# Linear attention and a gated feed-forward on one core: scores and tiled outputs of two batches in one stretch, halves in steps 1 and 2, later planned landings, last rows in two parts

## The chip, the core and the metric

The kernel runs on one core of a Trainium2 chip. Its engines have instruction streams of their own: PE (matrix products, TensorE), ACT (ScalarE), DVE (VectorE), POOL (GpSimd) and SP (SyncE, which here only starts transfers). PEld in the profile is PE's loading of weights. The metric is device time in microseconds (us); lower is better. Eight runs of the kernel before lie between 198.23 and 200.33 us, with a median of 199.31.

## What is computed

```python
B, H, S, D = 4, 8, 768, 48          # q, k, v, f_logit: [B, H, S, D]
f = sigmoid(f_logit)
for t in range(S):
    state = f[:, :, t, :, None] * state + einsum('bhd,bhe->bhde', k[:, :, t], v[:, :, t])
    y[:, :, t] = einsum('bhd,bhde->bhe', q[:, :, t], state)
x = y.transpose(0, 2, 1, 3).reshape(B * S, H * D)            # 3072 x 384
out = (maximum(x @ w_gate, 0) * (x @ w_val)) @ w_out         # hidden width 1536
```

## The kernel before

**Tiling.** The sequence is cut into six steps of 128 tokens (`c`, 0 to 5). In a step each of the four batches is a unit of attention, and two batches form a pair (`pr`, 0 or 1). The recurrence is computed by blocks: sums of log f over the tokens of a step (`cum`, L659 and L662; L573 and L593 in step 0), exponentials of them on ACT (L669, L671), scaled k and q ("hats", L696 and L699 on POOL), their transposes `qkT` (on PE, L710, with a DVE copy L715 in steps 1 and 2; by a transposing DMA, L718, from step 3 on), scores k·q (L739), the causal mask (`ptm`, L744 on DVE), the output rows (L766 or L772/L776) and the new state (L800, then L548 on DVE and L550 on POOL).

**Two kinds of small-tile stretches on PE.** Scores contract over 48 rows, and heads are stored at row 0 and row 64, so a batch's eight score matmuls alternate between the two halves of PE's rows and fill two banks of PSUM. The "tiled" outputs of steps 0 to 2 (`intra`, L766) write 32 partitions at a time: 16 matmuls per batch, plus 12 with the old state from step 1 on. They give the outputs already transposed, as the feed-forward wants them. From step 3 on (`natural`) the outputs are 128 rows wide and a transposing DMA (L791) turns them.

**Feed-forward.** For each of twelve blocks of hidden units (`j`) `ffn_hidden` computes gate and value, three matmuls each (L829); ACT takes relu of the gate (L835), DVE multiplies (`gT`, L839). A triple of three matmuls is 512 columns wide, or 256 where `halves` splits the four batches: for the first six `j` of step 0 each half of the batches has triples of its own. `ffn_out` multiplies twelve blocks of `gT` by w_out (L852, 384 columns), ACT evicts (L862), SP stores 128 rows (L866).

**What sets the order.** Nothing is placed by hand. Every operation is put into a plan with the tiles that it reads and writes, an assumed cost (`occ`, `lat`) and a priority. `schedule` takes, again and again, the operation that can start first (priority breaks ties) and so makes a fixed order for each engine; it also deals out the eight PSUM banks, at most so many of a kind (four of "f" for the feed-forward, four of "s" for scores, two of "y"). `settle` repeats this eight times, and between the rounds `transfers` plays the two DMA queues (SP's and POOL's) packet by packet to get a planned landing for each load. On the chip each engine works its list in order and waits on semaphores. Planned times thus decide only who stands behind whom. `dma` (L446) holds what `transfers` needs: packets and ns per packet, alone and beside the other queue. Attention comes before feed-forward by priority, and chains (`chain`, L513) keep scores, outputs, transposes and feed-forward matmuls each in their own order.

**Transfers.** SP loads f, k, q, v, one pair at a time (384 KB each); POOL starts the loads of w_gate, w_val and w_out in three parts each (L494), which also convert to bf16. The list `first` (L318) fixes the first of them: `wo0@q1.0` lets part 0 of w_out start only when q of step 1, pair 0 has landed; `f1.0@wv1` holds that f until part 1 of w_val has landed. Part s of w_out is read by the s-th four of the twelve L852 matmuls of a row block.

**Filling.** In the first 15 us PE gets idle matmuls (L912) on planned gaps.

Of the kernel before, what the change touches and what calls it, by code (L numbers as in the profile page):

```python
# [42 lines left out]
class Plan:  # L43
# [140 lines left out]
    def transfers(self):  # L184
# [9 lines left out]
        for op in rings["POOL"]:  # L194
            queue["POOL"].append([op, op.parts[0], op.start + 3.0])
# [24 lines left out]
        while True:  # L220
            feed()
            heads = {e: queue[e][0] for e in queue if queue[e]}
            if not heads:
                break
            can = {e: h for e, h in heads.items() if h[2] <= t}
            if not can:
                times = [h[2] for h in heads.values()]
                if nxt < len(sp) and pending is None:
                    times.append(max(sp[nxt].ready, issue["SP"]))
                t = max(t + 0.01, min(times))  # L230
                continue
            e = next(iter(can)) if len(can) == 1 else ("POOL" if last == "SP" else "SP")
            h = can[e]
            t += h[0].parts[1 if len(can) == 1 else 2] / 1000.0
            last = e
            h[1] -= 1
            if e == "SP":
                sent += 1
            if h[1] == 0:
                h[0].land = t + (0.6 if e == "SP" else 1.6)  # L240
                queue[e].pop(0)
# [58 lines left out]
def bass_hgrn2_outer__then__ffn_reglu_kernel(  # L300
# [12 lines left out]
    halves = {0: 6}  # L313
    dec_dma = set()
    x_way = {0: "tiled", 1: "tiled", 2: "tiled", 3: "xbar", 4: "xbar", 5: "xbar"}
# [5 lines left out]
    C = 128  # L321
# [30 lines left out]
    dec = [sb(f"dec{i}", [128, B // 2, 2, 2, NP], F32) for i in range(NA)]  # L352
    NW = 2
    drow = sb("drow", [128, NW, D, 2, 2, NP], F32)
# [31 lines left out]
    def pe_t(*cols):  # L386
        return sum({256: 0.124}.get(n, n / 2400.0 + 0.0045) for n in cols)
# [58 lines left out]
    def dma(op, slot, flow, parts, n=1):  # L446
# [5 lines left out]
        op.flow, op.parts = flow, (n * parts[0], parts[1], parts[2])  # L452
# [31 lines left out]
    def load_w(nm, s, after):  # L484
# [12 lines left out]
        dma(op, f"{nm}{s}", 2.45, (32, 62, 62) if nm == "wo" else (24, 80, 80))  # L497
# [40 lines left out]
    def new_state(kv, c, b, w, P):  # L538
        ai = c % NA
        s_old, s_new = st[b][(c + 1) % 2], st[b][c % 2]  # L540
        rate = dec[ai][:, b // 2, :, b % 2, :].rearrange("q j p -> q p j").unsqueeze(3).to_broadcast([128, NP, 2, D])
# [11 lines left out]
    def attention_pair(c, b0):  # L553
# [43 lines left out]
        for j in range(2):  # L597
            lo = 64 * j
            add("ACT", lambda lo=lo, j=j: sc.activation(
                dec[ai][lo:lo + 64, b0 // 2, j, :, :].rearrange("p b n -> p n b"),  # L600
# [39 lines left out]
    def attention_front(c, b):  # L640
# [17 lines left out]
        def cum():  # L658
            mm = te.matmul(bc.ap[:, 0:HD], tri[:, :], bn[:, :, 0:D])  # L659
            if c < NC - 1 and c not in dec_dma:  # L660
# [4 lines left out]
        chain("cum", "PE", cum, ["tri", "ones", f"bneg{bi}", f"bn{bi}_{bj}"], [bc], occ=0.28 if c < NC - 1 and c not in dec_dma else 0.17,  # L665
# [7 lines left out]
        if c in dec_dma:  # L673
            wi = w // 2 % NW
            add("ACT", lambda: sc.activation(drow[96:128, wi, :, :, bj, :].rearrange("q d j p -> q p j d"),
                                             bc.ap[96:128, 0:HD].rearrange("q (p j d) -> q p j d", p=NP, j=2), AF.Exp, scale=-1.0),
                [bc], [f"drow{wi}_{bj}"], prio=P + 2, **act_t(HD))
            if bj:
                def copies():
                    row, cell = NW * 2 * HD, 2 * B * NP  # L680
                    return [sy.dma_start(
                        bass.AP(tensor=dec[ai], offset=64 * j * cell + (b // 2) * 4 * NP + j * 2 * NP, ap=[[cell, D], [1, 2 * NP]]),
                        bass.AP(tensor=drow, offset=127 * row + wi * 2 * HD + j * 2 * NP, ap=[[row, 1], [4 * NP, D], [1, 2 * NP]]))
                        for j in range(2)]
                op = add("SP", copies, [f"drow{wi}_{i}" for i in range(2)] + [f"dec{ai}"],
                         [f"dec{ai}_{b_}{j}{hh}" for b_ in (b - 1, b) for j in range(2) for hh in range(2)], occ=0.9, lat=1.2, prio=P + 5)
                dma(op, f"dec{ai}_{b // 2}", 0.2, (3, 16, 24), 2)
        elif c < NC - 1:
            for j in range(2):
                lo = 64 * j  # L690
                add("ACT", lambda lo=lo, j=j: sc.activation(dec[ai][lo:lo + 64, b // 2, j, bj, :], bc.ap[lo:lo + 64, HD:HD + NP], AF.Exp,
# [31 lines left out]
    def attention(c, b):  # L723
        w = c * B + b
        P = w * 10
        hi, qi, mi, vi = w % NH, w % NQ, w % NM, w % NV
        xi = c % NX
        vp = vpad[vi]
        vin = ld["v"][:, slot_of("v", c, b // 2), b % 2, :, :]
        vout = bass.AP(tensor=vp, offset=0, ap=[[VW, 128], [VSTEP, NP], [64, 2], [1, D]])  # L730
        add("POOL", lambda: gp.tensor_copy(vout, vin.rearrange("p (n j) d -> p n j d", j=2)),  # L731
            in_keys("v", c, b, b + 1) + [f"vpad{vi}"], [f"v_{vi}"], prio=P + (55 if c in twos else 3), **pool_c(HD))
        sA, sB = Bank("s"), Bank("s")

        def scores():
            for p in range(NP):
                for j, s in ((0, sA), (1, sB)):
                    lo = 64 * j
                    mm = te.matmul(s.ap[:, p * C:(p + 1) * C], tokens(c, b, 1, p, lo, lo + D), tokens(c, b, 0, p, lo, lo + D))  # L739
            return mm  # L740
        chain("scores", "PE", scores, qk_(qi), [sA, sB], occ=0.34, lat=PE_L, prio=P + 5, opens=[sA, sB])
        mask = tri[:].unsqueeze(1).to_broadcast([128, NP, C])
        for j, s in ((0, sA), (1, sB)):
            add("DVE", lambda j=j, s=s: ve.tensor_tensor(  # L744
                ptm[mi][:, j, :, :], s.ap[:, :].rearrange("p (n t) -> p n t", n=NP), mask, ALU.mult),
                [s, "tri"], [f"ptm{mi}_{j}{hh}" for hh in range(2)], prio=P + 6, **dve_t(512))

        y = Bank("y")
        s_old = st[b][(c + 1) % 2]
        s_key = [f"S{b}_{(c + 1) % 2}"] if c else []  # L750

        def intra():
# [6 lines left out]
            for r in range(NK):  # L759
                rounds.append([(n, vp[:, p * VSTEP + 32 * i + 16 * (i == 2):p * VSTEP + 32 * i + 16 * (i == 2) + 32],  # L760
                                ptm[mi][:, i // 2, p, :]) for n, (p, i) in list(enumerate(blocks))[4 * r:4 * r + 4]])
            rounds.append([(3 * p + 1, vp[:, p * VSTEP + 48:p * VSTEP + 80], ptm[mi][:, 1, p, :]) for p in range(NP)])
# [7 lines left out]
        def natural():  # L770
# [3 lines left out]
            for h in range(H):  # L774
                at = h // 2 * VSTEP + h % 2 * 64
                mm = te.matmul(y.ap[:, h * D:(h + 1) * D], ptm[mi][:, h % 2, h // 2, :], vp[:, at:at + D],  # L776
                               start=False, stop=True, skip_group_check=True)
            return mm
        x_key = [f"xT{xi}_{b}"]
        need = qk_(qi) + [f"v_{vi}", *(f"ptm{mi}_{j}{hh}" for j in range(2) for hh in range(2))] + s_key  # L780
        if x_way[c] == "tiled":
            yop = chain("intra", "PE", intra, need + [f"vpad{vi}"], [y], occ=0.52 if c else 0.38, lat=PE_L, prio=P + 7, opens=[y])
            add("ACT", lambda: sc.activation(xT[xi][:, :, b * C:(b + 1) * C],  # L783
                                             y.ap[:, 0:HD].rearrange("p (n t) -> p n t", n=NK), AF.Copy),
                [y], x_key, prio=P + 8, **act_t(HD))
        else:
            chain("intra", "PE", natural, need, [y], occ=0.38, lat=PE_L, prio=P + 7, opens=[y])
            ni = w % NN
            add("ACT", lambda: sc.activation(xn[ni][:, :], y.ap[:, 0:HD], AF.Copy), [y], [f"xn{ni}"], prio=P + 8,
                **act_t(HD))  # L790
            op = add("SP", lambda: sy.dma_start(xT[xi][:, :, b * C:(b + 1) * C], xn[ni][:, :], transpose=True),  # L791
                     [f"xn{ni}"], x_key, prio=P + 8, occ=1.3, lat=1.2)
            dma(op, f"xT{xi}_{b}", 0.6, (24, 20, 28))

        def rest():
            kv = Bank("kv")

            def state():
                for p in range(NP):
                    mm = te.matmul(kv.ap[:, p * 96:(p + 1) * 96],  # L800
                                   hats[:, hi, 1, 2 * p:2 * p + 2, :].rearrange("p h d -> p (h d)"),
                                   bass.AP(tensor=vp, offset=p * VSTEP, ap=[[VW, 128], [64, 2], [1, D]]))
                return mm
            if c in twos:
                attention_back(c, b, behind[-1])
            chain("state", "PE", state, hk_(hi) + [f"hats{hi}", f"v_{vi}"], [kv],
                  occ=0.18, lat=PE_L, prio=P + (32 if c in twos else 6), opens=[kv])
            new_state(kv, c, b, w, P + (25 if c in twos else 0))
        if c in twos:
            behind.append(yop)  # L810
            later.append(rest)
        elif c < NC - 1:
            rest()
# [28 lines left out]
    OJ = 4  # L842

# [28 lines left out]
    for c in range(NC):  # L872
# [5 lines left out]
        for b in range(B):  # L878
            if c not in twos and b % 2 == 0:
                attention_front(c, b)  # L880
                attention_front(c, b + 1)
            elif b % 2 == 0:
                attention_pair(c, b)
            attention(c, b)
# [13 lines left out]
    for item in pend:  # L898
        ffn_out(*item)

# [102 lines left out]
```

## Time and profile before

| | us |
|---|---|
| median of 8 runs | 199.31 |
| lowest, highest | 198.23, 200.33 |
| the profiled execution | 199.21 |
| its span, first to last instruction | 197.5 |
| busy in it: PE, PEld | 186.2, 102.4 |
| busy in it: ACT, DVE, POOL | 111.1, 105.4, 76.2 |
| eight score matmuls, mean duration of one | 0.218 |
| four maskings in a row on DVE, at 20.92 us | 2.48 |

The span is what the trace shows; the rest of an execution lies around it. Matmuls overlap: the duration of one is longer than its share of PE's time, so the share is read from start to next start. The DMA engines are busy through most of the first 134 us:

```profile
0.00:5.00 5.00, 3.45 (x9) 1.05 (x10) 3.71 (x13) 1.50 (x2) 3.96 (x17) 1.00 0.51 138
30.00:36.20 6.20, 3.97 (x29) 2.10 (x30) 2.75 (x6) 4.62 (x15) 2.84 (x4) 1.00 1.04 199
36.20:62.00 25.80, 25.80 (x333) 15.18 (x334) 15.85 (x27) 17.02 (x38) 17.95 (x23) 1.00 1.11 213
91.00:134.00 43.00, 43.00 (x349) 23.01 (x349) 21.91 (x34) 26.29 (x56) 17.82 (x22) 1.00 0.94 187
134.00:186.60 52.60, 52.60 (x334) 26.93 (x333) 22.11 (x33) 23.19 (x43) 4.83 (x6) 1.00 0.28 72
```

Each row is a stretch of the span: its length, the busy time (and number of instructions) of PE, PEld, DVE, ACT and POOL, the granted TensorE clock, the busy share of the DMA engines and GB/s.

### The profile page before, as it was taken

The numbers are of one execution on the slowest core, as the hardware profiler recorded it, in microseconds if no ns is written. First come the engines' busy times: TensorE is split into PE (matmuls) and PEld (weight loads), VectorE is DVE, ScalarE is ACT, GpSimd is POOL, SyncE is SP. The second block draws the span as 40 slices with busy tenths as digits, with TensorE's granted clock in tenths as the row PEclk, the third lists the DMA queues.
The fourth block names the chain that finished last, engine by engine and source line by source line (L and its number), as shares of the span: only waits on it lengthen the run. The fifth ranks groups of instructions, "written<-read, shape, count | busy, mean of one in ns | idle before, by whom it ended". The sixth has DMA issues, their size and how long they took to land.

```text
span 197.5 us, 4253 instructions
## 1 busy us (share of the span) xinstructions
PE 186.2 (94%) x1705; PEld 102.4 (52%) x1705; DVE 105.4 (53%) x183; ACT 111.1 (56%) x237; POOL 76.2 (39%) x108
## 2 busy tenths in 40 slices
PE   6874997799999999999999999999999999999994
PEld 2443784356655554556455555544545555544562
DVE  7755874574819786576566455446247232443300
ACT  2776439671587768856646876377434434344311
POOL 8276002976286829594640652904500000000000
PEclk9999999999999999999999999999999999999999
DMA  4999999999999989997899979999562210111112
GB/s 136 272 271 205 206 194 204 182 206 216 221 208 242 204 174 219 193 230 150 191 174 186 236 169 181 210 194 228 106 132 62 61 40 0 43 40 40 40 75 84
DMA packets 118051, 31.73 MB, mean 161 GB/s; under 512 B 111120, under 2 KB 118032, under 8 KB 118032
## 3 DMA queue, kind: packets, MB, share of 16 engines
q1 hardware_dynamic: 114048, 27.93, 66.3%
q0 software_dynamic: 3984, 3.54, 11.1%
q8 instruction: 13, 0.21, 0.4%
q14 instruction: 6, 0.05, 0.1%
HBM read 25.95 MB, written 4.72 MB: 155 GB/s over the span
## 4 chain that ended last, share of the span: by engine, by line
PE 80%; issue 8%; POOL 5%; DMA 3%; SPq 2%; ACT 0%; POOLq 0%
PE ps L829 43%; PE ps L852 24%; PE ps L739 3%; DMA f_in<-in_f_logit_dram 3%; PE ps L766 2%; PE ps L710 2%; SPq L474 2%; PE ps L659 2%; PE ps L800 2%; POOL wg L494 1%; PE ps L776 1%; POOL wv L494 1%; PE ps L772 1%; POOL vpad L731 1%; PE ps L662 1%
## 5 line engine op out<-in xcount | busy, mean ns | idle before, releaser
L839 DVE TENSOR_TENSOR gT<-relu,ps 128x512 bf16<-128x512 bf16 (+1 forms) x78 | 49.8, 644 | 58.3 <-PE ps L829 47.8
L835 ACT ACTIVATE relu<-ps 128x512 bf16<-128x512 f32 (+1 forms) x78 | 43.7, 563 | 30.2 <-PE ps L829 29.9
L829 PE MATMUL ps<-xT,wv 128*128 128x512 bf16 (+1 forms) x234 | 59.5, 363 | 1.1 <-DMA wv<-in_moe_w_val_dram 1.1
L829 PE MATMUL ps<-xT,wg 128*128 128x512 bf16 (+1 forms) x234 | 59.4, 363 | 0.6 <-DMA wg<-in_moe_w_gate_dram 0.6
L852 PE MATMUL ps<-wo,gT 128*128 128x384 bf16 x288 | 51.4, 326 | 0.0
L744 DVE TENSOR_TENSOR ptm<-ps,tri 128x512 bf16<-128x512 f32 x48 | 30.9, 683 | 11.7 <-PE ps L739 11.7
L852 PEld LDWEIGHTS ps<-wo,gT 128*128 128x128 bf16 x288 | 27.0, 98 | 18.7
L829 PEld LDWEIGHTS ps<-xT,wg 128*128 128x128 bf16 x234 | 21.7, 98 | 20.3 <-issue 0.7
L829 PEld LDWEIGHTS ps<-xT,wv 128*128 128x128 bf16 x234 | 21.1, 98 | 20.8 <-DMA wv<-in_moe_w_val_dram 1.4
L696 POOL TENSOR_TENSOR hats<-k_in,expo 128x384 bf16<-128x384 f32 x20 | 19.9, 1002 | 27.4 <-ACT expo L669 15.4
L862 ACT ACTIVATE osb<-ps 128x384 f32<-128x384 f32 x24 | 11.8, 491 | 31.3 <-PE ps L852 31.3
L699 POOL TENSOR_TENSOR hats<-q_in,expo 128x384 bf16<-128x384 f32 x20 | 19.9, 1000 | 1.9 <-DMA q_in<-in_q_dram 1.9
L550 POOL TENSOR_TENSOR st<-ssum,dec 128x384 bf16<-128x384 f32 x16 | 13.6, 847 | 10.7 <-DVE ssum L548 10.7
L731 POOL CAST vpad<-v_in 128x384 bf16<-128x384 f32 x24 | 11.9, 507 | 4.5 <-DMA v_in<-in_v_dram 4.5
L669 ACT ACTIVATE expo<-ps 128x384 f32<-128x384 f32 x20 | 9.8, 490 | 3.8 <-PE ps L662 3.0
L650 ACT ACTIVATE f_in<-f_in 128x768 f32<-128x768 f32 x10 | 8.4, 840 | 4.0 <-DMA f_in<-in_f_logit_dram 4.0
L548 DVE TENSOR_TENSOR ssum<-ps,st 128x384 f32<-128x384 f32 x16 | 8.8, 552 | 3.3 <-PE ps L800 2.9
L739 PE MATMUL ps<-qkT 48*128 48x128 bf16 x192 | 9.2, 218 | 0.9 <-ACT qkT L617 0.9
L671 ACT ACTIVATE expo<-ps 128x384 f32<-128x384 f32 x20 | 9.8, 488 | 0.0
L739 PEld LDWEIGHTS ps<-qkT 48*128 48x128 bf16 x192 | 5.4, 94 | 7.9 <-issue 5.0
L783 ACT ACTIVATE xT<-ps 128x384 bf16<-128x384 f32 x12 | 5.9, 490 | 5.0 <-PE ps L766 4.9
L715 DVE COPY qkT<-ps 128x1024 bf16<-128x1024 bf16 x8 | 5.5, 690 | 5.7 <-PE ps L710 5.7
(73 smaller groups left out, 143.2 us busy)
## 6 DMA issues: line engine op xcount, KB each, us to landing
f_in<-in_f_logit_dram SPq DMA_DIRECT2D x12, 384.0 KB, 5.1
k_in<-in_k_dram SPq DMA_DIRECT2D x12, 384.0 KB, 5.3
q_in<-in_q_dram SPq DMA_DIRECT2D x12, 384.0 KB, 6.0
v_in<-in_v_dram SPq DMA_DIRECT2D x12, 384.0 KB, 5.4
out_dram<-osb SPq DMA_DIRECT2D x24, 192.0 KB, 2.4
wg<-in_moe_w_gate_dram POOLq DMA_DIRECT2D x3, 384.0 KB, 8.0
wv<-in_moe_w_val_dram POOLq DMA_DIRECT2D x3, 384.0 KB, 9.2
wo<-in_moe_w_out_dram POOLq DMA_DIRECT2D x3, 384.0 KB, 7.9
```

Of the source, the lines that this page charges most:

```text
L550: add("POOL", lambda: gp.tensor_tensor(t4(s_new), t4(tmp), rate, ALU.mult), [key] + dk, [f"S{b}_{c % 2}"], prio=P + 8, **pool_t(HD))
L669: add("ACT", lambda: sc.activation(ex[:, 1, :], bc.ap[:, 0:HD], AF.Exp, scale=1.0), [bc], [f"expk{ei}"], prio=P + 1, **act_t(HD))
L696: add("POOL", lambda: gp.tensor_tensor(hk, kin[:, b % 2, :, :], ex[:, 1, :].rearrange("p (h d) -> p h d", h=H), ALU.mult), in_keys("k", c, ...
L699: add("POOL", lambda: gp.tensor_tensor(hq, qin[:, b % 2, :, :], ex[:, 0, :].rearrange("p (h d) -> p h d", h=H), ALU.mult), in_keys("q", c, ...
L731: add("POOL", lambda: gp.tensor_copy(vout, vin.rearrange("p (n j) d -> p n j d", j=2)), in_keys("v", c, b, b + 1) + [f"vpad{vi}"], [f"v_{v ...
L739: mm = te.matmul(s.ap[:, p * C:(p + 1) * C], tokens(c, b, 1, p, lo, lo + D), tokens(c, b, 0, p, lo, lo + D))
L744: add("DVE", lambda j=j, s=s: ve.tensor_tensor(ptm[mi][:, j, :, :], s.ap[:, :].rearrange("p (n t) -> p n t", n=NP), mask, ALU.mult), [s, " ...
L829: mm = te.matmul(bank.ap[:, 0:n], wt[:, kt, j * 128:(j + 1) * 128], xT[xi][:, kt, n0:n1], start=(kt == 0), stop=(kt == NK - 1))
L835: add("ACT", lambda: sc.activation(relu[ri][:, 0:n], gate.ap[:, 0:n], AF.Relu), [gate], [f"relu{ri}"], prio=P, **act_t(n))
L839: add("DVE", lambda: ve.tensor_tensor(gT[gi][:, j, n0:n1], relu[ri][:, 0:n], val.ap[:, 0:n], ALU.mult), [val, f"relu{ri}"], [f"gT{gi}_{j}_ ...
L852: mm = te.matmul(o[b].ap[:, 0:DM], gT[gi][:, j, b * C:(b + 1) * C], wo[:, j, :], start=(j == 0), stop=(j == NJ - 1))
L862: add("ACT", lambda b=b, oi=oi: sc.activation(osb[oi][:, :], o[b].ap[:, 0:DM], AF.Copy), [o[b]], [f"osb{oi}"], prio=P, **act_t(DM))
```

## The change

`attention` takes both batches of a pair. For the pairs in `s_twin` (all but the first pairs of steps 0 and 1) their sixteen score matmuls are one operation that opens four banks; for those in `y_twin` ((1,1), (2,0), (2,1)) the tiled outputs of both batches are one operation with two banks. Which pairs have tiled outputs stays the same. `halves` now covers steps 1 and 2 too. In the plan, landings on SP's queue are put 1.0 or 1.9 us after the last packet (before 0.6), POOL's transfers begin 2.2 or 2.9 us after their start (before 3.0), wo's packets take 80 ns beside the other queue (before 62), and PE's assumed costs are a table. The rows of the last batch of the last step go through `ffn_end`: columns 0 to 255, then 256 to 383, each with its own bank, eviction and store. A path for decays by DMA, used in no step, is removed, and `dec` is laid out so that the decays of one batch lie together.

```diff
-            queue["POOL"].append([op, op.parts[0], op.start + 3.0])
+            queue["POOL"].append([op, op.parts[0], op.start + op.parts[3]])
...
-                h[0].land = t + (0.6 if e == "SP" else 1.6)
+                h[0].land = t + (1.6 if e == "POOL" else 1.0 if h[0].ready < 1.0 else 1.9)
...
-    halves = {0: 6}
-    dec_dma = set()
-    x_way = {0: "tiled", 1: "tiled", 2: "tiled", 3: "xbar", 4: "xbar", 5: "xbar"}
+    halves = {0: 6, 1: 6, 2: 6}
+    x_way = {(c, pr): "tiled" if c < 3 else "xbar" for c in range(6) for pr in range(2)}
+    s_twin = {(c, pr) for c in range(6) for pr in range(2)} - {(0, 0), (1, 0)}
+    y_twin = {(1, 1), (2, 0), (2, 1)}
...
-        return sum({256: 0.124}.get(n, n / 2400.0 + 0.0045) for n in cols)
+        return sum({128: 0.0566, 256: 0.109, 384: 0.1627, 512: 0.2162}[n] for n in cols)
...
-        dma(op, f"{nm}{s}", 2.45, (32, 62, 62) if nm == "wo" else (24, 80, 80))
+        dma(op, f"{nm}{s}", 2.45, (32, 62, 80, 2.2) if nm == "wo" else (24, 80, 80, 2.9))
...
-    def attention(c, b):
...
-        chain("scores", "PE", scores, qk_(qi), [sA, sB], occ=0.34, lat=PE_L, prio=P + 5, opens=[sA, sB])
+    def attention(c, bs):
+        units = []
...
+        for part in ([units] if (c, bs[0] // 2) in s_twin else [[u] for u in units]):
+
+            def scores(part=part):
+                for b, w, s in part:
+                    for p in range(NP):
+                        for j in range(2):
+                            lo = 64 * j
+                            mm = te.matmul(s[j].ap[:, p * C:(p + 1) * C], tokens(c, b, 1, p, lo, lo + D),
+                                           tokens(c, b, 0, p, lo, lo + D))
+                return mm
+            at = [s for _, _, ss in part for s in ss]
+            chain("scores", "PE", scores, [t for _, w, _ in part for t in qk_(w % NQ)], at, occ=0.21 * len(part) + 0.22, lat=PE_L,
+                  prio=part[0][1] * 10 + 5, opens=at)
...
+        for part in ([units] if tiled and (c, bs[0] // 2) in y_twin else [[u] for u in units]):
+            ys = [Bank("y") for _ in part]
+
+            def rows(part=part, ys=ys):
+                return [(intra if tiled else natural)(u, y) for u, y in zip(part, ys)][-1]
+            op = chain("intra", "PE", rows, [t for u in part for t in need(u) + ([f"vpad{u[1] % NV}"] if tiled else [])], ys,
+                       occ=(0.34 if c else 0.19) * len(part) + 0.235 if tiled else 0.38, lat=PE_L, prio=part[0][1] * 10 + 7, opens=ys)
...
+    def ffn_end(g, b, cols):
+        gi, oi = g % NG, (g * B + b) % NO
+        P = (g + 1) * B * 10 + 5 + NJ * 3 + b * 3
+        for i, (n0, n1) in enumerate(cols):
+            o = Bank("f")
+
+            def part(o=o, n0=n0, n1=n1):
+                for j in range(NJ):
+                    mm = te.matmul(o.ap[:, 0:n1 - n0], gT[gi][:, j, b * C:(b + 1) * C], wo[:, j, n0:n1], start=(j == 0),
+                                   stop=(j == NJ - 1))
+                return mm
...
-        for b in range(B):
-            if c not in twos and b % 2 == 0:
+        for b in range(0, B, 2):
+            if c in twos:
+                attention_pair(c, b)
+            else:
                 attention_front(c, b)
                 attention_front(c, b + 1)
-            elif b % 2 == 0:
-                attention_pair(c, b)
-            attention(c, b)
+            attention(c, (b, b + 1))
...
-    for item in pend:
+    for item in pend[:-1]:
         ffn_out(*item)
+    ffn_end(NC - 1, B - 1, [(0, 256), (256, DM)])
```

## The prediction

> **What bounds the kernel now.** First the page: does one engine fill the span, and where not?
>
> ```profile
> span 197.5 us, 4253 instructions
> PE 186.2 (94%) x1705; PEld 102.4 (52%) x1705; DVE 105.4 (53%) x183; ACT 111.1 (56%) x237; POOL 76.2 (39%) x108
> PE   6874997799999999999999999999999999999994
> PEclk9999999999999999999999999999999999999999
> ```
>
> PE is full from about the eighth slice (8 x 4.94 = 39 us) to the end, at full clock; the others are about half busy. Holes are only in the head. Second, the chain that ended last, in order of time (start, length, what):
>
> ```profile
> 18.29 15.04 issue
> ...
> 33.34 0.81 POOL wo L494
> 34.16 1.01 POOL hats L696
> 35.17 0.95 POOL hats L699
> 36.17 0.62 PE ps L710 x8
> ...
> 186.80 7.81 PE ps L852 x48
> 194.64 0.49 ACT osb L862
> ```
>
> Until 36.17 POOL decides: it stands still until q of step 1, pair 0 has landed (the waits give 15.05 us to that DMA), issues wo part 0 and makes two hats, and PE starts step 1's transposes. From there the chain is PE alone to 194.64, and the PE waits after 36.2 us list no other wait at all. So the time is: head (36.17), plus every PE slot after it (158.5), plus a tail of 2.85 (eviction 0.49, store issue 0.33, landing 1.8, the end). The profiled execution took 199.21, 1.72 more than its span; the median of eight is 199.31, so the sum needs no shift.
>
> Third, the PE timeline, for what a slot costs. I read start to next start, not the durations, since matmuls overlap:
>
> ```profile
> 20.39 0.63 PE L739 MATMUL ps<-qkT 48*128 48x128 bf16 x16
> 20.95 0.50 PE L829 MATMUL ps<-xT,wg 128*128 128x256 bf16 x3
> ...
> 38.09 0.81 PE L829 MATMUL ps<-xT,wg 128*128 128x512 bf16 x3
> 38.84 0.40 PE L739 MATMUL ps<-qkT 48*128 48x128 bf16 x8
> 39.17 0.34 PE L659 MATMUL ps<-bneg,tri 128*128 128x384 bf16 x1
> ```
>
> Three 512-wide matmuls take 0.648 in a row, but 0.75 before scores: 0.10 is lost on entering. Eight scores take 0.33, sixteen 0.56: eight more cost 0.23, so 0.10 of the 0.33 is lost on leaving. Tiled outputs (L766) show the same: 12 in 0.175, so 16 should take 0.233, yet they take 0.33; entering costs 0.09. I call this a switch, 0.097 mean.
>
> **Part 1: scores of two batches together, tiled outputs of two together.** In the instruction order of the two kernels I count entries and exits of the two kinds of small-tile stretches: 65 before, 42 after. Scores go from 20 stretches of 8 and two of 16 to two of 8 and eleven of 16; outputs of (1, pair 1) and both pairs of step 2 merge. The matmuls are the same. 23 fewer switches x 0.097 = **2.23 us** off PE, all behind 47 us, where PE is full. The Trainium skill has a rule for this (TensorEngine Tiling (Array Packing), Key Properties): changing the tiling mode drains TensorE. It gives no price; as an estimate, TensorE: Matmul & The Clock Gate, Single matmul latency, puts an isolated 128-wide warm matmul at (398+128)/2.4 = 219 ns, 163 more than the 56 of a streamed one (eight transposes take 0.45), so 23 switches would bring 3.7 us. The trace has its own row for a switch, so I take 2.23.
>
> The cost side is DVE. Both batches' scores fill four banks, and their four maskings (L744) are placed in one run nearly everywhere: four took 2.48 us at 20.92, two took 1.29. Behind them on DVE queue the products into gT (L839), which free PE's banks. A rule speaks against the change here: the tiling page, PSUM Bottleneck, warns that faster tiles leave evacuation as the limit. By the rule each twin is worth DVE's 2.48, not PE's 0.56 + 0.10. By the trace, DVE is idle 47% of the time, and what counts is the PE work placed behind the scores. Worst place: step 1, pair 1. The first gT can start 0.53 (scores to masking) + 2.4 + 0.5 (a state sum) = 3.4 us after the scores start; PE has 0.56 + 0.17 (state) + 0.54 (sums) + 7 x 0.327 = 3.56 us of work to the point at which four products are open. So it just fits. Elsewhere 1.95 us blocks of w_out follow, needing no DVE. Bounds for all twins: 0 to 9 x 0.3 = 2.7; below nothing is excluded, since no row lets a longer burst free a bank earlier. I take **+0.5**, near the place worked out.
>
> **Part 2: halves for steps 1 and 2.** 72 matmuls of 512 columns become 144 of 256: 48 x 0.327 - 24 x 0.648 = **+0.15** on PE. ACT and DVE each get 12 more instructions: 12 x (2 x 0.382 - 0.596) = 2.0 and 12 x (2 x 0.415 - 0.686) = 1.7 us, beside PE; their cover is the idle half, and what it costs when gone is in the burst bounds above. It also lets step 1's hidden layer start with two batches instead of four (before: last xT at 56.2, first use at 56.86).
>
> **Part 3: later planned landings, new PE costs.** These only reorder. In the head, PE gets two more half triples and a full one ahead of step 1's sums, and in all three more full triples ahead of its transposes (3 x 0.648 = 1.95 us net), where before it stood 1.36 (29.22 to 30.91, less 0.33) and 1.47 us (34.05 to 36.17, less 0.65). ACT lets one more relu pass before the exponential that waits for f (landing at 29.0). POOL's gate is the same transfer: SP's first 17 issues are unchanged, wv part 1 (landing 14.06 + 9.2 = 23.2) still releases them, so the transposes still start at about 36.17. POOL puts a vpad before wg part 0 (into its 1.35 us of waiting) and a hats before wv part 2, whose use is far off: nothing.
>
> So 1.95 would be gained, but what is late next? The w_out matmuls now come earlier. The landings of wo parts 0, 1, 2 are 33.3+6.3, 36.5+7.9, 37.3+9.7 = 39.6, 44.4, 47.0. Adding slots from 36.17 in the new order, PE reaches part 1 at 43.94 (waits 0.46) and part 2 at 46.3 (waits 0.7): it goes on at 47.0, where before it was at the same point at 47.80. Of 1.95 only **0.80** stays. This also swallows any small stall in the head up to 1.15.
>
> SP: the first two stores of step 0 move ahead of k and q of step 2, and SP waits for their eviction (48.3, 48.9). k then goes out at about 49.7 (before 46.81), q at 51.2 (48.30), v at 52.8 (53.40), f of pair 1 at 56.4 (53.91). With landings of 6.4 and 6.1 (the k and q rows at 46.8 and 48.3) q is there at 57.3, its hats done by 59; PE wants them at 59.6. Covered by 0.6 us. Later loads fall within 2 us of the old ones while PE's score stretches come 1 to 4 us later than before.
>
> **Part 4: last rows in two parts.** 12 x 384 columns (1.95) become 12 x 256 and 12 x 128: 1.31 + 0.68 = 1.99, +0.03. The last eviction shrinks from 0.49 to about 0.27 (256 columns take 0.38, so 0.11 less per 128); the first store's issue (0.33) is over before the second is ready. The smaller transfer may land 0.1 sooner than 1.8. **-0.28** in all.
>
> **Sum.** 199.21 - 2.23 + 0.5 + 0.15 - 0.80 - 0.25 (tail with its PE cost) = **196.6**.
>
> **Rivals.** *B, wo does not bind* (0.12): its parts land 1.2 us earlier, since the queues run differently. Then all of the 1.95 stays: 195.4. Against it: POOL issues them at the same gate and the same loads compete. *C, the DVE burst decides* (0.15): each twin costs PE 0.3: 196.6 - 0.5 + 2.7 = 198.8, no measurable change. For it: 2.48 us against banks for about 2.6 us of hidden layer. Against: in the old kernel DVE waits 47.8 us for L829's matmuls, PE none for DVE. *D, stores ahead of loads* (0.13), the slower one: q of step 2 behind two stores lands late, and step 2's first transposes stop PE. The price is each us of landing past 58.5. From 3.6 us (landing 10.9 after issue) it outweighs everything by more than 0.5%. Rows of 12.6 (q) and 11.6 (v) exist, issued at 34.2 and 36.7 beside wo parts 1 and 2; at 12.6 PE stops for 5.2: 201.8. Against: without wo beside them, loads took 4.6 to 6.9, once 9.2. That switches do not vanish at all is excluded by the 0.56 for sixteen.
>
> My forecast has 0.60, its own range 195.6 to 198.2. 0.5%, about what a measurement can tell here, is 1.0 us: faster means below 198.3. Faster: 0.57 + 0.12 + 0.05 of C = 0.74; same: 0.13; slower: 0.13. The range takes in B and most of C.
>
> **What would show it.** Scores: eleven stretches of 16, 0.56 to the next start. PE goes on at 36.2, with two waits for wo near 44 and 46.5 of about 1.1 together; B if they are absent. gT and PE waits: PE waiting on DVE in the four stretches before 90 us points to C. PE waiting at L694 near 59 us on POOL, and POOL on q, is D. The last eviction row: 128x128 at about 0.27. I am wrong if PE's waits after 47 us add up to more than 1.5 us.

## The result, and the profile after

The changed kernel takes **197.18 us** (median of 11 runs, 196.21 to 197.75), beside 199.34 for the kernel before on the same chips: a ratio of 0.9877, 95% interval 0.9854 to 0.9899. It ran once more later, with three experiments: 195.56 us beside 198.80, ratio 0.983 (0.9804 to 0.9856). So one kernel moves by 0.5% from one such comparison to the next against the same kernel before. Ratios are reckoned from the runs within 1.5% of the fastest of their kernel, while medians and ranges hold the few slower ones too, so a ratio is not the quotient of the printed medians. Numbers below are compared inside one group of runs on one chip where they can be, and differences under about 1 us between groups are not read.

Line numbers have moved (before, after): scores L739, L724; tiled outputs L766, L759; transposes L710, L694; maskings L744, L734; hidden layer L829, L834; its product L839, L844; w_out L852, L877 (the last rows L857); state L800, L810; the q hats L699, L683.

The profiled execution took 196.54 us. Its page, first part (busy time and number of instructions of each engine, then tenths in 40 slices):

```profile
span 194.8 us, 4465 instructions
PE 185.9 (95%) x1790; PEld 111.8 (57%) x1790; DVE 105.7 (54%) x195; ACT 111.7 (57%) x250; POOL 76.0 (39%) x108
PE   6977999896999999999999999999999999999995
PEclk9997999999999999999999999999999999999999
```

PE is as full as before, and the span is 2.7 us shorter. Two things are new: a PE slice of 6 tenths at 43.8 to 48.7 us, and one slice (14.6 to 19.5 us) with a lower granted clock. The chain that ended last (start, length, what) names the first:

```profile
18.55 14.81 issue
...
34.17 1.01 POOL hats L680
37.31 10.17 DMA wo<-in_moe_w_out_dram
47.53 3.42 PE ps L877 x20
...
184.64 5.85 PE ps L877 x36
190.49 1.99 PE ps L857 x24
```

Before, POOL's hats led straight into PE's transposes and from there PE was never released by another engine. Now part 2 of w_out, issued at 37.31, ends the chain's head: PE's stream begins to set the end only at 47.53. PE's timeline at the places that the prediction named (start, duration, engine, line, what; in brackets the idle time before it):

```profile
36.19 0.62 PE L694 MATMUL ps<-ident,hats 128*128 128x128 bf16 x8 [0.83 <-POOL hats L683]
...
45.03 1.47 PE L877 MATMUL ps<-wo,gT 128*128 128x384 bf16 x8 [0.99 <-DMA wo<-in_moe_w_out_dram]
...
47.53 0.66 PE L877 MATMUL ps<-wo,gT 128*128 128x384 bf16 x3 [0.53 <-DMA wo<-in_moe_w_out_dram]
...
53.90 0.62 PE L724 MATMUL ps<-qkT 48*128 48x128 bf16 x16
54.45 0.34 PE L810 MATMUL ps<-vpad,hats 128*128 128x96 bf16 x4
...
57.16 0.49 PE L834 MATMUL ps<-xT,wg 128*128 128x256 bf16 x3
57.56 0.50 PE L834 MATMUL ps<-xT,wv 128*128 128x256 bf16 x3
```

The transposes start where they did. Two waits for w_out follow, 1.52 together. Sixteen scores take 0.55 from start to next start. At 57.16 a half triple takes 0.40 instead of 0.33: 0.07 is all that PE loses behind the burst of four maskings, which is here on DVE:

```profile
54.56 2.48 DVE L734 TENSOR_TENSOR ptm<-ps,tri 128x512 bf16<-128x512 f32 x4 [0.88 <-PE ps L724]
56.96 0.55 DVE L547 TENSOR_TENSOR ssum<-ps,st 128x384 f32<-128x384 f32 x1
57.43 1.07 DVE L844 TENSOR_TENSOR gT<-relu,ps 128x256 bf16<-128x256 bf16 x3
```

The first product that frees a bank starts 3.53 us after the scores did; the prediction had 3.4. At the end of the span the two parts follow each other (ACT evicts, SPq issues the stores):

```profile
190.33 2.14 PE L857 MATMUL ps<-wo,gT 128*128 128x256 bf16 x24
191.84 0.39 ACT L862 ACTIVATE osb<-ps 128x256 f32<-128x256 f32 x1 [0.82 <-PE ps L857]
192.25 0.90 SPq L865 DMA_DIRECT2D out_dram<-osb  x2
192.51 0.28 ACT L862 ACTIVATE osb<-ps 128x128 f32<-128x128 f32 x1 [0.28 <-PE ps L857]
```

PE ends at 192.47 and the span at 194.8: 2.3 us of tail, 0.5 less than before. From the transposes to PE's end it is 156.28 us, where it was 158.47. That difference of 2.19 can be put together from slots. Triples moved ahead of the transposes take 1.95 away, and 23 fewer switches in that stretch (55 to 32 by the trace) take 2.23 at the prediction's price. Coming back are 1.66 at w_out (the two waits with 0.14 that the slots beside them lengthen), 0.07 behind the burst, 0.25 at L810 near 114 us, and 0.18 of halves and last rows. The sum is -2.02; 0.17 is left over.

### The profile page after: what moved, and what is told of

Read it like the earlier page. It is cut to its first block, busy times and chain, and to the rows that moved or that the text cites. A ratio compares the mean times of both kernels' runs of the same rounds, so it can differ in the third digit from the quotient of the medians.

```text
span 194.8 us, 4465 instructions
## 1 busy us (share of the span) xinstructions
PE 185.9 (95%) x1790; PEld 111.8 (57%) x1790; DVE 105.7 (54%) x195; ACT 111.7 (57%) x250; POOL 76.0 (39%) x108
## 4 chain that ended last, share of the span: by engine, by line
PE 69%; DMA 11%; issue 8%; POOL 6%; SPq 4%; ACT 1%; POOLq 0%
PE ps L834 37%; PE ps L877 21%; DMA q_in<-in_q_dram 6%; DMA wo<-in_moe_w_out_dram 5%; SPq L473 4%; PE ps L724 2%; POOL hats L683 1%; PE ps L694 1%; PE ps L759 1%; PE ps L810 1%; PE ps L658 1%; PE ps L857 1%; PE ps L771 1%; POOL vpad L714 1%; PE ps L767 1%
## 5 line engine op out<-in xcount | busy, mean ns | idle before, releaser
L844 DVE TENSOR_TENSOR gT<-relu,ps 128x512 bf16<-128x512 bf16 (+1 forms) x90 | 51.0, 577 | 52.6 <-PE ps L834 40.5
L840 ACT ACTIVATE relu<-ps 128x512 bf16<-128x512 f32 (+1 forms) x90 | 45.7, 511 | 30.1 <-PE ps L834 29.5
L834 PE MATMUL ps<-xT,wg 128*128 128x512 bf16 (+1 forms) x270 | 62.2, 340 | 0.0
L834 PE MATMUL ps<-xT,wv 128*128 128x512 bf16 (+1 forms) x270 | 61.9, 338 | 0.0
L877 PE MATMUL ps<-wo,gT 128*128 128x384 bf16 x276 | 49.5, 326 | 1.5 <-DMA wo<-in_moe_w_out_dram 1.5
L877 PEld LDWEIGHTS ps<-wo,gT 128*128 128x128 bf16 x276 | 25.9, 98 | 18.8 <-DMA wo<-in_moe_w_out_dram 1.9
L834 PEld LDWEIGHTS ps<-xT,wg 128*128 128x128 bf16 x270 | 25.5, 99 | 17.7
L834 PEld LDWEIGHTS ps<-xT,wv 128*128 128x128 bf16 x270 | 24.9, 98 | 18.0 <-DVE ssum L547 0.2
L734 DVE TENSOR_TENSOR ptm<-ps,tri 128x512 bf16<-128x512 f32 x48 | 30.5, 683 | 8.6 <-PE ps L724 8.5
L887 ACT ACTIVATE osb<-ps 128x384 f32<-128x384 f32 x23 | 11.3, 491 | 29.6 <-PE ps L877 29.4
L683 POOL TENSOR_TENSOR hats<-q_in,expo 128x384 bf16<-128x384 f32 x20 | 19.8, 1002 | 8.1 <-DMA q_in<-in_q_dram 8.1
L699 DVE COPY qkT<-ps 128x1024 bf16<-128x1024 bf16 x8 | 5.5, 689 | 10.2 <-PE ps L694 10.0
L649 ACT ACTIVATE f_in<-f_in 128x768 f32<-128x768 f32 x10 | 8.4, 842 | 4.2 <-DMA f_in<-in_f_logit_dram 4.2
L724 PEld LDWEIGHTS ps<-qkT 48*128 48x128 bf16 x192 | 5.4, 94 | 5.5 <-issue 1.8
L724 PE MATMUL ps<-qkT 48*128 48x128 bf16 x192 | 7.7, 217 | 0.9 <-ACT qkT L616 0.9
```

Of the source, the lines that this page charges most:

```text
L683: add("POOL", lambda: gp.tensor_tensor(hq, qin[:, b % 2, :, :], ex[:, 0, :].rearrange("p (h d) -> p h d", h=H), ALU.mult), in_keys("q", c, ...
L724: mm = te.matmul(s[j].ap[:, p * C:(p + 1) * C], tokens(c, b, 1, p, lo, lo + D), tokens(c, b, 0, p, lo, lo + D))
L734: add("DVE", lambda mi=mi, j=j, s=s: ve.tensor_tensor(ptm[mi][:, j, :, :], s.ap[:, :].rearrange("p (n t) -> p n t", n=NP), mask, ALU.mult) ...
L834: mm = te.matmul(bank.ap[:, 0:n], wt[:, kt, j * 128:(j + 1) * 128], xT[xi][:, kt, n0:n1], start=(kt == 0), stop=(kt == NK - 1))
L840: add("ACT", lambda: sc.activation(relu[ri][:, 0:n], gate.ap[:, 0:n], AF.Relu), [gate], [f"relu{ri}"], prio=P, **act_t(n))
L844: add("DVE", lambda: ve.tensor_tensor(gT[gi][:, j, n0:n1], relu[ri][:, 0:n], val.ap[:, 0:n], ALU.mult), [val, f"relu{ri}"], [f"gT{gi}_{j}_ ...
```

## The experiments

Twelve kernels in three groups of four, each group on one chip (1, 2 and the version by hand of 8; 3, 4, the first of 7 and the second of 8; the rest); the kernel before had medians of 199.57, 198.86 and 198.80 in them.

**1. No stretches of two batches.** Everything else as changed, the plan made anew; 66 switches again.

```diff
-    s_twin = {(c, pr) for c in range(6) for pr in range(2)} - {(0, 0), (1, 0)}
-    y_twin = {(1, 1), (2, 0), (2, 1)}
+    s_twin = set()
+    y_twin = set()
```

> The changed kernel with no pair in s_twin and y_twin, all else as it is; planned anew. In its instruction order PE has 66 switches of tile shape against 42. Theory (a switch costs PE 0.097 us wherever it stands): 24 x 0.097 = 2.3 us more than the changed kernel, 199.5 us, with about the same waits for wo near 44 and 47 us. Rival 1 (the gain came from the planning, the twins only shorten what waits anyway): within 0.7 us of the changed kernel's 197.2. Rival 2 (the burst of four maskings costs PE): less than 1.5 us more, with waits of PE on DVE gone that the changed kernel has.

Measured: 199.14 us (197.50 to 200.69), ratio 0.9961 (0.9932 to 0.999). Only 0.4% of gain is left. The control of experiment 2, the changed kernel but for ten small matmuls, took 196.57 on the same chip, 2.6 us less, where the theory had 2.3. Rival 1 (0.7 at most) is out: even the near ends of the two intervals lie 0.9 us apart. Rival 2 has nothing to stand on, since behind 36 us the changed kernel loses 0.07 to maskings. One part of the theory failed: PE waits for w_out only once here, 0.19 us at 46.42.

**2. The price of a switch by itself.** The order is that of the changed kernel; in each stretch one extra matmul of zeros with 64 columns stands between the two batches, into a bank that the scores then overwrite. On 128 rows it leaves the small tile shape and comes back; on 48 rows, as a control, it does not.

```diff
-                for b, w, s in part:
+                for n, (b, w, s) in enumerate(part):
+                    if n:
+                        te.matmul(s[0].ap[:, 0:64], zeros[:, 0:128], zeros[:, 0:64])
```

(control: `zeros[0:48, 0:128], zeros[0:48, 0:64]`)

> The changed kernel with one full-size matmul of 64 columns put between the two batches of each twin of scores (ten places, nine of them behind 36 us); it writes zeros that the next score matmul overwrites, and the instruction order of every engine is otherwise that of the changed kernel. Theory (a switch costs 0.097): 9 x (2 x 0.097 + 0.029) = 2.0 us more, 199.2 us, and from the start of a twin to the next start 0.55 + 0.22 = 0.77. Rival (what a stretch costs is filling its first banks, not the change of shape): 0.3 us more, 197.5.

> Control for the run before: the same extra matmul of 64 columns at the same places, but over 48 rows, the shape of the scores. Theory: no switch, so only its own columns: 9 x 0.03 = 0.3 us more than the changed kernel, 197.5. Rival: as much more as with the full-size matmul (2.0).

Measured: 197.94 us (196.25 to 199.28), ratio 0.9905 (0.9873 to 0.9937), against 196.57 (195.52 to 198.59), 0.984 (0.9795 to 0.9886). Both are about 1 us under their expectation; between them lie 1.37 us where 1.7 were expected for the nine stretches behind 36 us. The two intervals overlap a little, so the price is read from the traces. One stretch in the timeline of the first:

```profile
66.80 0.40 PE L726 MATMUL ps<-qkT 48*128 48x128 bf16 x8
67.13 0.20 PE L722 MATMUL ps<-zeros 128*128 128x64 bf16 x1
67.26 0.40 PE L726 MATMUL ps<-qkT 48*128 48x128 bf16 x8
67.59 0.82 PE L836 MATMUL ps<-xT,wv 128*128 128x512 bf16 x3
```

And the same one in the control:

```profile
64.55 0.40 PE L726 MATMUL ps<-qkT 48*128 48x128 bf16 x8
64.78 0.19 PE L722 MATMUL ps<-zeros 48*128 48x64 bf16 x1
64.79 0.41 PE L726 MATMUL ps<-qkT 48*128 48x128 bf16 x8
65.13 0.82 PE L836 MATMUL ps<-xT,wv 128*128 128x512 bf16 x3
```

From 66.80 to 67.59 it takes 0.79 us, against 0.58 in the control, which has the same 64 columns, and 0.55 for the sixteen in one stretch. So 0.21 goes for two switches: 0.105 for one, where the prediction had 0.097. The extra matmul in the small shape adds 0.03; what costs is the change of shape.

**3. The new plan alone.** The kernel before with the planned landings, w_out's packet time and PE's costs of the changed one; no stretches of two, halves in step 0 only, last rows whole.

```diff
-            queue["POOL"].append([op, op.parts[0], op.start + 3.0])
+            queue["POOL"].append([op, op.parts[0], op.start + op.parts[3]])
...
-                h[0].land = t + (0.6 if e == "SP" else 1.6)
+                h[0].land = t + (1.6 if e == "POOL" else 1.0 if h[0].ready < 1.0 else 1.9)
...
-        return sum({256: 0.124}.get(n, n / 2400.0 + 0.0045) for n in cols)
+        return sum({128: 0.0566, 256: 0.109, 384: 0.1627, 512: 0.2162}[n] for n in cols)
...
-        dma(op, f"{nm}{s}", 2.45, (32, 62, 62) if nm == "wo" else (24, 80, 80))
+        dma(op, f"{nm}{s}", 2.45, (32, 62, 80, 2.2) if nm == "wo" else (24, 80, 80, 2.9))
```

> The kernel before with the new planned landings, wo packet time and PE costs alone: stretches, halves and last rows as before. Theory: the order in the head changes as in the changed kernel, 1.95 us of triples more ahead of the transposes, but PE then reaches parts 1 and 2 of w_out early and waits there 1.1 to 1.6 us: 0.3 to 0.8 us off 199.3, so 198.5 to 199.0. Rival, wo does not bind: 197.4. Rival, a reordering is worth nothing without the stretches: 199.3 or more.

Measured: 198.94 us (197.63 to 200.79), ratio 0.9989 (0.9963 to 1.0015): nothing that can be told from no change. PE's waits (engine, line, released by: us in total, times, longest; three of the rows) are not those expected:

```profile
PE ps L766 <- DVE ptm L744: 1.4, 2, 0.8
PE ps L829 <- ACT xT L783: 0.6, 1, 0.6
PE ps L710 <- POOL hats L699: 0.5, 1, 0.5
```

There is no wait for w_out at all. Instead PE waits 0.63 at 45.15 for maskings and 0.60 at 55.44 for the first 512-wide triple of step 1, whose xT needs the last tiled output of the step. (The other 0.8 of the first line lies at 15 us, as before.) My reading, which no run isolates: with the triples that were moved into the head, less of step 0 is left to stand between step 1's scores and outputs. The traced execution took 197.89, 1 us under this kernel's median, so its waits alone do not account for the median either.

**4. The changed kernel without halves in steps 1 and 2.**

```diff
-    halves = {0: 6, 1: 6, 2: 6}
+    halves = {0: 6}
```

> The changed kernel with halves in step 0 only; steps 1 and 2 have 512-wide triples. Theory: the halves cost PE 0.15 us and no wait, so without them 197.0, no difference that can be told from the changed kernel's 197.2. Rival: the halves cover the maskings of four banks (step 1's hidden layer can begin with two batches); without them PE waits by 0.5 us or more, 197.7 to 198.5, at the scores of steps 1 and 2.

Measured: 199.31 us (198.19 to 201.73), ratio 0.9994 (0.997 to 1.0018). The theory, no difference, is refuted, and the rival came with more than its price (0.5 to 1.3): the whole gain is gone. On the same chip a kernel that differs from the changed one in its last rows only (experiment 7) took 195.99, 3.3 us less (3.2 over the runs that the ratios count). PE's timeline after step 1, pair 1's scores:

```profile
53.60 0.24 PE L661 MATMUL ps<-ones,bneg 128*128 128x1 bf16 x4
55.63 0.51 PE L759 MATMUL ps<-qkT,st 128*32 128x128 bf16 x12 [1.79 <-DVE ptm L734]
...
56.67 0.65 PE L759 MATMUL ps<-ptm,vpad 128*32 128x128 bf16 x16
58.30 1.46 PE L834 MATMUL ps<-xT,wg 128*128 128x512 bf16 x3 [0.98 <-ACT xT L788]
59.55 1.06 PE L694 MATMUL ps<-ident,hats 128*128 128x128 bf16 x8
60.41 1.49 PE L834 MATMUL ps<-xT,wv 128*128 128x512 bf16 x3
```

In the changed kernel twelve half triples stand around the sums and directly behind the outputs (54.63 to 60.22). Here nothing stands there: PE waits 1.79 us for the burst of four maskings and 0.98 for xT. And then it is slow: three 512-wide matmuls take 1.25 from start to next start instead of 0.65, eight transposes 0.86 instead of 0.44, with a granted clock of 0.62 in the mean of 53.5 to 62.5 us. From 55.63 to 62.78 PE's slots without the wait took 6.17, at full clock they are 3.46. So the waits cost 2.77, the clock 2.7 more in this execution. Over the runs that the ratio counts, four with a mean clock of 1.0 lie at 198.19 to 199.83, three with 0.974 at 199.91 to 201.01. So most of the gain is gone at full clock too: the mean of those four, 198.75, is 2.8 us above 195.99.

**5. Is it the burst, or the lack of work?** The same, and step 1, pair 1 goes batch by batch again, in scores and outputs.

```diff
-    halves = {0: 6, 1: 6, 2: 6}
+    halves = {0: 6}
...
-    s_twin = {(c, pr) for c in range(6) for pr in range(2)} - {(0, 0), (1, 0)}
-    y_twin = {(1, 1), (2, 0), (2, 1)}
+    s_twin = {(c, pr) for c in range(6) for pr in range(2)} - {(0, 0), (1, 0), (1, 1)}
+    y_twin = {(2, 0), (2, 1)}
```

> The changed kernel without halves in steps 1 and 2, and with the scores and tiled outputs of step 1, pair 1 batch by batch. Theory now: PE runs out of step 0's hidden layer there, and only halves let step 1's begin before the last output; without them PE waits 0.6 us for maskings and 0.6 to 1.0 for xT at 53 to 58 us, with or without the stretch of two batches: 198.2 to 198.8. Rival: the burst of four maskings alone makes the wait, so it goes when that pair goes batch by batch: 4 switches more (0.4), 0.15 less on PE, 197.4.

Measured: 197.27 us (196.28 to 197.94), ratio 0.9915 (0.9884 to 0.9946). The number is the rival's, but both numbers had been reckoned from 197.2 for the changed kernel; beside it on the same chip (195.56) the difference is 1.7 us, a little over the theory's 1.0 to 1.6. The timeline gives each a part:

```profile
54.83 0.40 PE L759 MATMUL ps<-ptm,vpad 128*32 128x128 bf16 x16
55.83 0.82 PE L834 MATMUL ps<-xT,wg 128*128 128x512 bf16 x3 [0.60 <-ACT xT L788]
```

The wait for maskings went with the burst (the rival was right there), and so did the loss of clock; the wait of 0.60 for xT stays. With four switches (0.39) and without the halves' 0.15 that makes 0.84 of the 1.7; waits of 0.54 for a transposing DMA and 0.47 for vpad at 92 and 113 us stand in this trace too, and I have not separated them from what changes from execution to execution.

**6. Halves in step 1 only**, 512-wide triples in step 2 (`halves = {0: 6, 1: 6}`).

> The changed kernel with halves in steps 0 and 1 and 512-wide triples in step 2. Theory: the cover is needed at step 1 only, so the time is that of the changed kernel in this job less 0.07, no difference to be measured. Rival: step 2's halves cover its maskings and its xT as well; without them PE waits by 0.5 us or more at 70 to 90 us.

Measured: 196.21 us (195.51 to 197.22), ratio 0.9869 (0.9839 to 0.9899), 0.65 us above the changed kernel beside it, with intervals that overlap. PE waits 0.30 for maskings at 75.9 and 0.16 for ACT behind it: the rival's mechanism, at just under its mark of 0.5. Step 1's halves are the ones that matter; step 2's are worth about half a microsecond by this trace, and the times do not tell that from nothing.

**7. The last rows in one part.**

```diff
-    for item in pend[:-1]:
+    for item in pend:
         ffn_out(*item)
-    ffn_end(NC - 1, B - 1, [(0, 256), (256, DM)])
```

> The changed kernel with its last rows in one part of 384 columns. Theory of the prediction: 0.28 us longer at the tail, 0.03 less on PE: 197.4. Rival, the measured tail (2.27 us against 2.85 before): 0.55 longer, 197.7, with 2.8 us from PE's end to the span's end. Rival, the tail is not on the path: 197.2.

> The last rows in one part once more, beside the changed kernel on one chip; the first measurement gave a ratio of 0.981 where the changed kernel had 0.988 elsewhere. Theory: the two parts are worth 0.28 to 0.55 us at the tail, so this is that much slower than the changed kernel of this job. Rival: the two parts cost something that the tail does not show, and this is 0.5 us or more faster again.

Measured: 195.99 us (194.83 to 197.80), ratio 0.981 (0.9766 to 0.9855); again, beside the changed kernel: 196.24 (194.85 to 197.25), 0.9867 (0.9831 to 0.9903), 0.7 us above its 195.56. The first went against both theories, the second with them in sign only, as the intervals overlap; the mean of the two ratios, 0.984, does not differ from the changed kernel's two, 0.985. In the traces the tail is plain: PE's end to the span's end is 2.84 and 2.86 us with one part, 2.3 and 2.4 with two. So half a microsecond is there, and the median of so few runs does not resolve it.

**8. w_out let go earlier.** First by hand: its three parts ahead of POOL's hats, part 0 released by k of step 1, pair 0 instead of its q; every other engine keeps its order. Then by the list, with the plan made anew.

```diff
+    w3, pool = [done[f"wo{i}"] for i in range(3)], order["POOL"]
+    first = pool.index(w3[0])
+    pool[:] = pool[:first] + w3 + [op for op in pool[first:] if op not in w3]
+    del w3[0].deps[done["q1.0"]]
+    w3[0].deps[done["k1.0"]] = "raw"
...
```

```diff
-    first = ("... f1.0@wv1 k1.0 q1.0 v1.0 wo0@q1.0 wo1 wo2 "
+    first = ("... f1.0@wv1 k1.0 q1.0 v1.0 wo0@k1.0 wo1 wo2 "
```

> The changed kernel with the three loads of w_out moved, after planning, to the front of POOL's first hats of step 1 and released by k of step 1, pair 0 (landing about 30) in place of q (33.4); every other engine keeps its order. Theory (wo's landing holds back 1.6 us at 44 and 47 us): both waits go, wo lands by 42, and the time falls by about 1.0, to 196.2, since q of that pair shares the DMA engines with wo and the first transposes of step 1 come up to 0.6 later. Rival (the DMA engines are full, so what wo gains q loses): the wait turns up at the transposes near 36 us as 1.5 us or more, and the time stays at 197.2 or rises.

> The changed kernel with w_out's part 0 let go when k of step 1, pair 0 has landed rather than its q, and the plan made anew for it. Theory: a load that gains here takes it from another in a full DMA; PE's waits at parts 1 and 2 (1.5 us) shrink, but f or q of step 1 come later by more than that, so 197.5 or more, up to the 203.9 of the move by hand, with a wait in 28 to 45 us. Rival: wo was simply let go too late, and the waits vanish: 195.7 to 196.5.

Measured: 203.87 us (202.46 to 204.73), ratio 1.0199 (1.0149 to 1.0248), by hand; 199.65 (197.97 to 202.12), 1.0017 (0.9996 to 1.0038), with the new plan. In both the waits for w_out are gone, and PE waits elsewhere for longer. By hand, once:

```profile
PE ps L834 <- ACT relu L840: 6.4, 1, 6.4
```

PE stands from 38.2 to 44.65 for a relu, and that relu stands on ACT behind the first operation on f of step 1, pair 1 (L649), which waited 8.60 us for its landing. The rival was right that the time rises, but the load that lost was this f and not q: the transposes started at 35.06. And by the new plan:

```profile
PE ps L694 <- POOL hats L683: 1.8, 3, 0.7
PE ps L759 <- DVE ptm L734: 1.4, 2, 0.8
PE ps L810 <- POOL vpad L714: 0.6, 2, 0.5
```

The three waits for hats lie at 56 to 68 us. POOL had stood still for 5.15 us until 45.91, for an exponential of the same f; that this is what makes the hats late is my reading, since POOL has short pauses in between. ACT takes that f at 35.97 us in the changed kernel, at 43.27 in the version by hand and at 42.59 in the planned one. In both, the three parts go out together at 30.6 or 30.7 us, where the changed kernel issues part 0 at 33.37 and the others at 36.5. The DMA engines are full there (a busy share of 1.22 from 28 to 37 us in both, 1.02 in the changed kernel). So what w_out gains in landing, f loses, and f has more behind it.

**9. The changed kernel again.**

> The changed kernel once more, unchanged, on the chip on which the next three run: it is what they are compared with. By the first measurement 0.988 of the kernel before, 196.6 to 197.3.

Measured: 195.56 us (194.89 to 196.12), ratio 0.983 (0.9804 to 0.9856). Its trace has no wait for w_out: the transposes start at 35.38 and PE goes through both parts at 43.16 and 45.20. In its place PE waits here:

```profile
PE ps L810 <- POOL vpad L714: 1.8, 2, 1.3
```

The first of the two is at 101.30, and POOL's vpad there had waited 3.8 us for v. So the trace of one execution is only one way in which loads can land. PE's lost time after 36 us is 2.0 us in the first trace and 2.3 in the second, at different places.

No version that was tried is measurably faster than the changed kernel.

## Why the prediction was right

The time was 197.18 (195.56 in the later runs, just under the range that began at 195.6), 196.6 was predicted, and 2.2 and 3.2 us were gained where 2.6 were forecast. The largest step was right. The other errors cancel in part, so that the sum came this close is partly luck. The steps, one by one:

- **Switches, -2.23: right.** The trace has 23 fewer behind 36 us, and experiment 2 measured one by itself at 0.105. The estimate from the Trainium skill's isolated latency, 163 ns, was too high by more than half. Its rule that a change of tiling mode drains TensorE fits; the drain itself no run here shows, only the price.
- **The burst of four maskings, +0.5: mis-sized**, 0.07 in this execution. The place and the arithmetic were right (3.4 us against 3.53, "it just fits"). The rule on PSUM eviction as the limit did not bite, but experiment 4 shows that this hangs on the half triples: without them the same burst costs 1.79 us, at the outputs that need the maskings, and behind that wait the clock was low.
- **Halves, +0.15: the term was right and its meaning was not.** On PE they cost that. But the prediction put what they cover into the bounds of the burst and treated the three parts as if they could be added. Halves and stretches can't: stretches without halves gain nothing (0.9994), or 0.85% once step 1, pair 1 goes batch by batch (0.9915), halves without stretches 0.4% (0.9961), the new plan without either 0.1% (0.9989), all together 1.2 to 1.7%. As I read it, the sum held because it was made on the whole order, in which the seven half triples already stood as cover.
- **Planned landings, -0.80: mis-sized**, -0.29 in the first trace: w_out's parts took 8.5 and 10.2 us to land instead of 7.9 and 9.7, so the waits were 1.66 with their surroundings, not 1.15. In the second trace they were absent, as rival B has it, and 1.78 us of waits for vpad came instead. By the prediction's own sign (more than 1.5 us of PE's waits after 47 us) it failed in that execution: the load that came late was not the one it had reckoned with. Alone, in experiment 3, the step measured 0.2 us (0.9989; the interval reaches to 0.7), and in its trace PE waited not for w_out but for maskings and xT at step 1's outputs (1.23 us).
- **Last rows, -0.25 with PE's part: mis-sized**, -0.5 by the traces. The last eviction was 0.28 (0.27 expected); the last transfer, now 64 KB, landed in 1.5 us where the one of 192 KB had taken 1.8, and I had taken 0.1 for that instead of 0.3. The prediction's own parts (0.22 and 0.1) also add up to 0.32, not 0.28.
- **SP, nothing: right.** The stores went ahead; q went out at the time reckoned (51.2), k 1.1 us after its 49.7:

```profile
48.91 1.82 SPq L891 DMA_DIRECT2D out_dram<-osb  x2
50.77 0.43 SPq L473 DMA_DIRECT2D k_in<-in_k_dram  x1
51.25 1.31 SPq L473 DMA_DIRECT2D q_in<-in_q_dram  x1
```

POOL makes q's hats at 58.4 and PE takes them at 60.22 without a wait. Rival D did not come.

In the profiled execution the terms are -2.23 (switches, count times price), +0.07 and +0.25 (burst, L810), +0.18 (halves and last rows on PE), -0.29 (landings) and -0.5 (tail), together -2.5; the two executions differ by 2.67. With experiment 2's 0.105 the switches would be -2.4, which closes the gap.

## What to carry to other kernels

The parts of a change to an engine that is nearly always busy cannot always be priced one at a time: joining work into longer stretches pays only if something else stands ready behind each stretch, so ask of each part which work covers it and whether another part has just moved that work away. Where the DMA engines are full, a wait at one load that an earlier start removes can come back at another, as in both versions of experiment 8, and the trace of a single execution does not tell which one will be late. A switch of matmul tile shape (0.1 us here) can be measured by one dummy matmul in the other shape, beside a control in the same shape.

## What the runs showed of the hardware

**A pause of PE of 1.8 us was followed by half the clock.** In experiment 4, 1.79 us without a matmul came before matmuls at half rate; without that pause, in experiment 5, every run had a mean clock of 1.0. The Trainium skill (TensorE: Matmul & The Clock Gate, HAM oscillation) puts the limit at idle gaps over about 3.4 us; here the clock fell behind a gap of half of that. It did not in every execution: of the runs that the ratio counts, three of 20 had a mean clock of 0.974 (the kernel before and the changed one were never below 0.982) and four had 1.0. In the changed kernel a gap of 0.99 at 45 us left the clock at 1.0. That the gap is the cause was not tested by itself. After the wait of 6.4 us in experiment 8, by hand, the clock was 0.50 from 44.6 to 49.0.

**In the head the clock differs between executions of the same program.** Stretch, length, busy time of PE, PEld, DVE, ACT and POOL, granted clock, DMA share and GB/s, of the changed kernel's first trace:

```profile
16.50:20.40 3.90, 3.85 (x28) 3.21 (x29) 1.57 (x3) 1.74 (x4) 2.04 (x4) 0.56 1.24 206
```

and of its second:

```profile
16.50:20.40 3.90, 3.20 (x46) 2.56 (x44) 1.66 (x5) 2.17 (x4) 1.72 (x4) 1.00 1.24 206
```

At 0.56 the half triples took 0.64 instead of 0.33. The kernel hides it, since it waits there for weights in any case: of the runs with mean clocks of 0.98 to 1.0, neither kind is the faster one (196.24 at 0.982, 197.38 at 1.0). What closes the gate in one execution and not in the next was not found.
